# Attention and two mixtures of experts on one core: row maxima split in place on GpSimd, all low weight parts on VectorE, third token tiles transposed whole

## The chip, the cores and the metric

The kernel runs on one core of a Trainium2 chip. The metric is the device time of one execution in microseconds (us), as the median of several runs. TensorE (PE in the profile; PEld is its weight load), VectorE (DVE), ScalarE (ACT), GpSimd (POOL) and SyncE (SP, which issues most DMAs) each work off a queue of their own in order and wait for each other through semaphores.

## The reference

```python
# 1. attention with decay: B=4 batches, 8 heads, 576 positions, 64 columns
cum = cumsum(log(clip(f, 1e-4, 1)))
scores = q @ k.T / 8 + (cum[:, None] - cum[None, :])        # per head, causal
attn = softmax(scores)                                      # with the row maximum subtracted
x = (attn @ v).reshape(2304, 512)
# 2. first mixture of experts: each token goes to its best expert
e = argmax(normalize(x) @ normalize(emb).T / tau);  gate = softmax(...)[e]
x = gate * (relu(x @ w1[e]) @ w2[e])
# 3. second one: (token, expert) pairs by descending logit, at most 288 tokens per expert
logits = x @ w_gate;  assign greedily
out = relu(x @ w1[e]) @ w2[e]
```

Products are done to about fp32 accuracy with pairs: an operand is held as a high part and a low part, and three products (high x high, low x high, high x low) are added up.

## The kernel before

**Attention.** There are 32 heads (batch times head). The loop over heads `n` has six steps `i` per head. In them TensorE does, interleaved: the scores of head n (`st_steps`, lines 545 and 546, into `px`), whose exponentials ScalarE writes (L547) and GpSimd masks (`affine_select`, L552 and L555); the scores of head n+1 once more, for its row maxima (`max_steps`, L509, into two buffers `pl`), which VectorE reduces (L513, L517); and the products with the values of head n-1 (`av_steps`, L578). When the maxima of head n+1 are complete, `rows1` splits them into a high and a low bf16 part in the tile `mb` (VectorE, L523 and L524); at the end of head n `rows` transposes `mb` on TensorE (five 128x128 transposes, L529, into `pr`), and ScalarE copies two rows of the result into rows 96 and 97 of the operand `opA` of head n+1 (L530). So the next head's scores subtract their maximum inside the product. Right behind the transposes TensorE starts the maxima of head n+2.

Operands are prepared two heads ahead by `prep`, in two halves: ScalarE copies a high part (`opA<-raw`, L469), GpSimd subtracts to get the low part (`opB<-raw,opA`, L470), and a DMA brings the high part into the other half of `opB` (L471). `parts` (L478 on VectorE, L480 on GpSimd) splits a transposed value tile every second head, and `ven` (L489) uses it behind the odd heads. In the text an odd head is one with `ven` behind its transposes.

**Experts.** `Weights.load` brings a piece of 128x1024 into one of four buffers `wraw` (SP), and `Weights.split` makes two parts of it: `whi` on ScalarE (L858) and `wlo`, by default on VectorE (L859). Each expert has 8 pieces, four for each of its two products. `load_next` issues the next load of a fixed list; as `wraw` has four buffers, a load waits on SP for the split of the piece four before it.

The first expert starts with the tokens whose place is known (`First`, L958, filled in while the router's last choices run), then `Experts.all` runs the eight experts of the first layer (room for 368, 368, 320, 312, 296, 280, 264 and 256 tokens) and later those of the second (288 each). Per expert there are 8 steps of the first product (L1558 into `pl`; ScalarE takes the positive part into `room_hh`, L1561; VectorE the rest into `room_hl`, L1562) and 4 of the second (L1582 into `py`). The tokens of the next expert are gathered by indirect DMA (POOL), at most 128 per tile, and transposed on TensorE beside the second product (`columns`, L1498); the third tile is transposed with its own number of rows (112, 64, 56, 40, 24, 8 or none in the first layer, 32 in the second). Beside an expert's steps the next expert's weights are split and the following ones loaded.

Some pieces of `wlo` go to GpSimd instead: eight around the first expert, and all eight that are made beside the last expert of the first layer for the first of the second:

```python
eng = self.nc.gpsimd if self.cold and p == E - 1 else None
...
W.split(0, 4 + j, self.nc.gpsimd if j % 2 else None)
```

**Between the layers** the second router's rounds (`Clear`) run: a chain of small VectorE operations (L1348 to L1374, ending in `c_cmp`), 20 small products (L1379) and two more VectorE operations. Three rounds are started early, beside the last expert; `finish` ends that expert (its logits, L1652); four rounds and the placing follow. Then GpSimd gathers the first expert's tokens of the second layer (L1785), TensorE transposes them (L874) and the second layer starts. The order of instructions on each engine is that of the code: nothing rearranges it.

## Time and profile before

| what | value |
|---|---|
| median of 3 runs | 843.05 us (835.38 to 844.14) |
| the profiled execution | 839.43 us, its span 837.5 us |
| busy: PE, PEld | 769.0 us (92%), 725.2 us (87%) |
| busy: DVE, ACT, POOL | 540.7 us (65%), 409.3 us (49%), 332.7 us (40%) |
| mean granted TensorE clock | 0.946 |

The stages by the clock of the span: attention to about 260 us, the first expert's start to 330, the first layer to 520, its last expert and the router's rounds to 592, the second layer to 830. Busy shares are averages over these: in the expert layers TensorE is never idle, in the others it is.

### The profile page before, as it was taken

How to read it: one execution, taken by the hardware profiler on the slowest of the kernel's cores; microseconds unless marked ns; L12 is line 12 of the kernel's file. 1: busy time of each engine (PE TensorE's matmuls, PEld its weight loads, DVE VectorE, ACT ScalarE, POOL GpSimd, SP SyncE). 2: the span in 40 equal slices, each digit the busy share in tenths (PEclk: the TensorE clock that was granted, in tenths of full speed). 3: DMA queues.
4: the chain of work that ended last, by engine and by line, in shares of the span. 5: the costliest groups of instructions: out<-in, count | busy, mean ns of one | idle time of the engine just before them, and what ended most of it. 6: DMA issues, size and time to landing. Idle time of an engine off the chain costs nothing. (4 is left out here: it accounts for less than half of the span.)

```text
span 837.5 us, 16417 instructions
## 1 busy us (share of the span) xinstructions
PE 769.0 (92%) x5813; PEld 725.2 (87%) x5813; DVE 540.7 (65%) x1362; ACT 409.3 (49%) x898; POOL 332.7 (40%) x659
## 2 busy tenths in 40 slices
PE   6899999999998798999999999654999999999995
PEld 2799999899898798999999999653799999999993
DVE  8888988858986668464565467866345554555530
ACT  5556656546656445455455567210344455454520
POOL 8686666546664737621132111810311312231011
PEclk8999999869999999999999999865899999999998
DMA  6466656536554436454555563520445655665410
GB/s 147 103 156 155 152 145 155 142 97 152 140 163 142 159 119 204 148 173 145 178 168 172 187 190 104 169 74 2 119 152 186 203 176 181 200 187 176 126 35 29
DMA packets 70256, 121.75 MB, mean 145 GB/s; under 512 B 29499, under 2 KB 38715, under 8 KB 70165
## 3 DMA queue, kind: packets, MB, share of 16 engines
q1 hardware_dynamic: 63924, 101.24, 43.0%
q0 software_dynamic: 6240, 19.36, 6.3%
q8 instruction: 50, 0.82, 0.4%
q14 instruction: 42, 0.34, 0.1%
HBM read 96.46 MB, written 14.63 MB: 133 GB/s over the span
## 5 line engine op out<-in xcount | busy, mean ns | idle before, releaser
L859 DVE TENSOR_TENSOR wlo<-wraw,whi 128x1024 fp32r<-128x1024 f32 x112 | 142.2, 1270 | 131.6 <-ACT whi L858 130.5
L858 ACT ACTIVATE whi<-wraw 128x1024 fp32r<-128x1024 f32 x128 | 134.6, 1056 | 4.3 <-DMA wraw<-v 3.6
L470 POOL TENSOR_TENSOR opB<-raw,opA 64x576 fp32r<-64x576 f32 x64 | 91.5, 1430 | 68.5 <-ACT opA L469 66.9
L1561 ACT ACTIVATE room_hh<-pl 128x288 fp32r<-128x288 f32 (+8 forms) x128 | 52.0, 406 | 106.3 <-PE pl L1558 105.8
L1558 PE MATMUL pl<-room_xh,whi 128*128 128x288 f32 (+7 forms) x512 | 94.4, 306 | 6.7 <-DVE room_hl L1562 6.2
L1562 DVE SCALAR_TENSOR_TENSOR room_hl<-pl,room_hh 128x288 fp32r<-128x288 f32 (+8 forms) x128 | 57.1, 448 | 53.9 <-ACT room_hh L1561 53.6
L1582 PE MATMUL py<-room_hh,wlo 128*128 128x288 f32 (+7 forms) x480 | 91.7, 315 | 0.0
L1558 PE MATMUL pl<-room_xl,whi 128*128 128x288 f32 (+7 forms) x512 | 90.2, 298 | 1.4 <-DVE room_xl L1501 1.4
L1558 PE MATMUL pl<-room_xh,wlo 128*128 128x288 f32 (+7 forms) x512 | 89.8, 297 | 0.0
L1558 PEld LDWEIGHTS pl<-room_xh,whi 128*128 128x128 f32 x512 | 75.7, 190 | 8.3 <-DVE room_hl L1562 7.4
L1558 PEld LDWEIGHTS pl<-room_xl,whi 128*128 128x128 f32 x512 | 76.0, 189 | 1.9 <-DVE room_xl L1501 1.7
L1582 PE MATMUL py<-room_hh,whi 128*128 128x288 f32 (+7 forms) x480 | 76.8, 303 | 0.0
L509 PE MATMUL pl<-opA 96*128 96x288 f32 (+2 forms) x192 | 70.6, 373 | 6.3 <-DVE opA L382 3.2
L1582 PE MATMUL py<-room_hl,whi 128*128 128x288 f32 (+7 forms) x480 | 76.4, 302 | 0.0
L1558 PEld LDWEIGHTS pl<-room_xh,wlo 128*128 128x128 f32 x512 | 76.0, 189 | 0.0
L545 PE MATMUL px<-opA 128*128 128x288 f32 (+2 forms) x192 | 74.1, 386 | 0.7 <-ACT opA L530 0.5
L1785 POOL DMA_INDIRECT xg<-y_d,ix x24 | 27.3, 1137 | 116.6 <-PE px L1498 86.1
L1582 PEld LDWEIGHTS py<-room_hh,wlo 128*128 128x128 f32 x480 | 71.2, 191 | 2.1
L513 DVE CUSTOM_DVE_ANT_0 mxs<-pl,mask 128x512 f32<-128x512 f32 (+3 forms) x128 | 61.8, 483 | 16.6 <-PE pl L509 12.8
L578 PE MATMUL py<-vv,room_hl 128*128 128x73 f32 x480 | 71.9, 274 | 0.0
L578 PE MATMUL py<-vv,room_hh 128*128 128x73 f32 x480 | 71.6, 270 | 0.0
L578 PEld LDWEIGHTS py<-vv,room_hl 128*128 128x128 f32 x480 | 69.6, 200 | 0.8
(369 smaller groups left out, 1527.4 us busy)
## 6 DMA issues: line engine op xcount, KB each, us to landing
wraw<-w SPq DMA_DIRECT2D x64, 512.0 KB, 3.6
wraw<-v SPq DMA_DIRECT2D x64, 512.0 KB, 3.5
raw<-qkT SPq DMA_DIRECT2D x32, 288.0 KB, 4.0
opB<-opA SPq DMA_DIRECT2D x64, 144.0 KB, 2.4
vv<-vrow SPq DMA_DIRECT2D x32, 160.0 KB, 3.1
vt<-vT SPq DMA_DIRECT2D x16, 288.0 KB, 4.0
x_d<-xr SPq DMA_DIRECT2D x16, 256.0 KB, 2.7
opA<-chl SPq DMA_DIRECT2D x60, 2.2 KB, 3.3
```

The lines of the kernel that those rows point to most:

```text
L470: nc.gpsimd.tensor_tensor(b_[lo, t, :], raw[:, t, :], r32(a[0:64, t, :]), op=ALU.subtract)
L509: nc.tensor.matmul(p[:, :wp], af[0:96, q0:q0 + 128], a[0:96, 1, k0:k0 + wp], start=True, stop=True)
L513: nc.vector.tensor_tensor_reduce(t[:qw, :w], p[:qw, :w], mask[:qw, m0:m0 + w], 1.0, mx[:qw, 5:6] if col == 4 else -3.0e38, op0=ALU.add, op ...
L545: nc.tensor.matmul(o, af[:, ks], a[:, 0, q1 - wp:q1], start=True, stop=False)
L578: nc.tensor.matmul(p[:, i, :], PT[n % 2][0][:, c:c + 128], v_[:, j, :], start=(k == 0), stop=(k == len(AORD) - 1))
L858: self.nc.scalar.activation(hi, raw, AF.Copy)
L859: (eng or self.nc.vector).tensor_tensor(lo, raw, r32(hi), op=ALU.subtract)
L1558: nc.tensor.matmul(o, a[:, d, f0:f0 + 128], b[:, d, o0:C], start=(n == 0), stop=(n == 11))
L1561: nc.scalar.activation(hh[:, fc, c0:C], o, AF.Relu)
L1562: nc.vector.scalar_tensor_tensor(hl[:, fc, c0:C], o, 0.0, r32(hh[:, fc, c0:C]), op0=ALU.max, op1=ALU.subtract)
L1582: nc.tensor.matmul(o, a[:, fc, :], b[:, fc, :C], start=(n == 0), stop=(n == 23))
L1785: nc.gpsimd.indirect_dma_start(out=g[:w], out_offset=None, in_=y_d, in_offset=IOA(ap=ix2[:w, p * NT + t:p * NT + t + 1], axis=0))
```

## The change

**Row maxima.** `mb` becomes a tile of fp32 (128x5x64, of which the bf16 view has 128 columns). VectorE writes each maximum into column 48 of it, so its high bf16 half stands in bf16 column 97; one GpSimd subtraction of 128x5 writes maximum minus high half, as bf16, over its low half in column 96. The two VectorE instructions L523 and L524 are dropped, and the rows of ones in `opA` change sign. The second half of `prep` moves from step 2 to step 4 of a head.

**Low parts.** `split` is divided in `upper` (ScalarE) and `lower` (VectorE), and no `wlo` is made on GpSimd any more. Beside the last expert of the first layer only four `upper` are made, without loads; their four `lower` come behind the rounds, right after the first gathers of the second layer, each with a load. The other four pieces of that expert are split in steps 0 to 3 of its first product.

**Third tiles** are transposed whole, 128x128, whatever their number of rows. One of them gets a memset of the rows that no gather has filled yet.

```diff
-    MB = [const.tile([128, NCH, 128], BF, name=f"mb{i}") for i in range(2)]
+    MB = [const.tile([128, NCH, 64], F32, name=f"mb{i}") for i in range(2)]
...
     def rows1(n):
-        mx, mb = MX[n % 2][:, 0:NCH], MB[n % 2]
-        nc.vector.scalar_tensor_tensor(mb[:, :, 96], mx, -2.0, mx, op0=ALU.mult, op1=ALU.add)
-        nc.vector.scalar_tensor_tensor(mb[:, :, 97], mx, -1.0, mb[:, :, 96], op0=ALU.mult, op1=ALU.subtract)
+
+        mx = MB[n % 2][:, :, 48:49]
+        nc.gpsimd.tensor_tensor(half(mx, 0), mx, half(mx), op=ALU.subtract)
...
-            nc.tensor.transpose(p[:, i * 128:(i + 1) * 128], MB[n % 2][:, i, :], identb)
+            nc.tensor.transpose(p[:, i * 128:(i + 1) * 128], MB[n % 2][:, i, :].bitcast(BF), identb)
...
-            if i in (0, 2):
+            if i in (0, 4):
                 emit(pp, 1)
...
-    first_expert.split(0, nc.vector)
+    first_expert.split(0)
     first_expert.split(1)
-    first_expert.split(2)
+    first_expert.W.upper(0, 2)
...
     first_expert.slots(u, EARLY // 128, NT)
+    first_expert.W.lower(0, 2)
...
-    def split(self, key, j, eng=None):
-        raw = self.raw.pop((key, j))
+    def upper(self, key, j):
         pool, k, bufs = (self.pool, "1", 4) if j < 4 else (self.pool2, "2", 8)
         hi = pool.tile([128, 1024], F32R, name="whi" + k, bufs=bufs)
         lo = pool.tile([128, 1024], F32R, name="wlo" + k, bufs=bufs)
-        self.nc.scalar.activation(hi, raw, AF.Copy)
-        (eng or self.nc.vector).tensor_tensor(lo, raw, r32(hi), op=ALU.subtract)
+        self.nc.scalar.activation(hi, self.raw[key, j], AF.Copy)
         self.parts[key, j] = (hi, lo)
 
+    def lower(self, key, j):
+
+        hi, lo = self.parts[key, j]
+        self.nc.vector.tensor_tensor(lo, self.raw.pop((key, j)), r32(hi), op=ALU.subtract)
+
+    def split(self, key, j):
+        self.upper(key, j)
+        self.lower(key, j)
+
...
-    def split(self, j, eng=None):
-        self.W.split(0, j, eng or self.nc.gpsimd)
+    def split(self, j):
+        self.W.split(0, j)
...
         for t, w in self.tiles(p):
-            nc.tensor.transpose(q[:, t * 128:t * 128 + w], self.rows[p][t][:w, d * 128:(d + 1) * 128],
-                                self.env["identf"][:w, :w])
+            nc.tensor.transpose(q[:, t * 128:(t + 1) * 128], self.rows[p][t][:, d * 128:(d + 1) * 128],
+                                self.env["identf"])
...
-            eng = self.nc.gpsimd if self.cold and p == E - 1 else None
+
+            last = self.cold and p == E - 1
...
-                    if self.cold and p == 0 and step in LATE:
-                        j = LATE.index(step)
-                        W.split(0, 4 + j, self.nc.gpsimd if j % 2 else None)
+                    if p == 0 and step in LATE:
+                        W.split(0, 4 + LATE.index(step))
                         load_next()
+                    if last and step % 2 == 1:
+                        nW.upper(np_, step // 2)
                     elif nW is not None and step % 2 == 1 and (p or not self.cold):
-                        nW.split(np_, step // 2, eng)
+                        nW.split(np_, step // 2)
                         load_next()
...
     L2 = Experts(nc, env, W2, (CAP,) * E, TAILS2, gather2, sink2, True, False)
     L2.fetch(0)
+
+    for j in range(4):
+        W2.lower(0, j)
+        load_next()
```

The order of GpSimd's instructions in two successive heads of the attention stage, the first an odd one; first before, then after. `mb` holds the maxima, `opB` the low operand parts, `room_h*` the exponentials.

```order
L480 TENSOR_TENSOR cum_118<-cum_118 128x576
L552 AFFINE_SELECT room_hl<-room_hl 128x2x128
L470 TENSOR_TENSOR opB_110<-raw,opA_107 64x576
L552 AFFINE_SELECT room_hl<-room_hl 128x2x128
L555 AFFINE_SELECT room_hl<-room_hl 64x64
L470 TENSOR_TENSOR opB_111<-raw,opA_108 64x576
```

```order
L480 TENSOR_TENSOR cum_118<-cum_118 128x576
L551 AFFINE_SELECT room_hl<-room_hl 128x2x128
L523 TENSOR_TENSOR mb_119<-mb_119 128x5
L551 AFFINE_SELECT room_hl<-room_hl 128x2x128
L470 TENSOR_TENSOR opB_110<-raw,opA_107 64x576
L554 AFFINE_SELECT room_hl<-room_hl 64x64
L470 TENSOR_TENSOR opB_111<-raw,opA_108 64x576
```

The split of the maxima comes between the two masks of 128x2x128, and the second `opB` of a head goes behind the second mask.

ScalarE's order in one head of the attention stage, from the copy of the transposed maxima to that of the next head, before and after. `room_hh<-px` are the exponentials, `opA<-raw` the two copies of `prep`.

```order
L530 ACTIVATE opA_107<-pr 2x576
L547 ACTIVATE room_hh<-px 128x288
L469 ACTIVATE opA_106<-raw 64x576
L547 ACTIVATE room_hh<-px 128x288
L547 ACTIVATE room_hh<-px 128x448
L469 ACTIVATE opA_106<-raw 64x576
L547 ACTIVATE room_hh<-px 128x320
```

```order
L546 ACTIVATE room_hh<-px 128x448
L546 ACTIVATE room_hh<-px 128x320
L626 ACTIVATE sq,ss_1200<-xr 128x448
L546 ACTIVATE room_hh<-px 128x192
L469 ACTIVATE opA_106<-raw 64x576
L546 ACTIVATE room_hh<-px 64x64
```

The second copy moves from behind the 448-column exponential to behind the 192-column one.

VectorE's order at the start of the second layer, from the end of the router's placing (`ix`) on, before and after. `room_xl` belongs to the first expert's tokens, `room_hl` to its first product.

```order
L1446 TENSOR_SCALAR ix_7747<-c_ut 128x24
L1463 UNCONDITIONAL_BRANCH x2
L1461 UNCONDITIONAL_BRANCH
L878 TENSOR_TENSOR room_xl<-px,room_xh 128x288 x2
L878 TENSOR_TENSOR room_xl<-py,room_xh 128x288 x2
L1562 SCALAR_TENSOR_TENSOR room_hl<-pl,room_hh 128x288 x2
L859 TENSOR_TENSOR wlo_8817<-wraw,whi_8816 128x1024
```

```order
L863 TENSOR_TENSOR wlo_7184<-wraw,whi_7183 128x1024
L887 TENSOR_TENSOR room_xl<-px,room_xh 128x288 x2
L887 TENSOR_TENSOR room_xl<-py,room_xh 128x288 x2
L1571 SCALAR_TENSOR_TENSOR room_hl<-pl,room_hh 128x288
L863 TENSOR_TENSOR wlo_8744<-wraw,whi_8743 128x1024
L1571 SCALAR_TENSOR_TENSOR room_hl<-pl,room_hh 128x288
L863 TENSOR_TENSOR wlo_8765<-wraw,whi_8764 128x1024
L863 TENSOR_TENSOR wlo_8771<-wraw,whi_8770 128x1024
L1571 SCALAR_TENSOR_TENSOR room_hl<-pl,room_hh 128x288
```

The first row after is the last of four `wlo` that now stand ahead of `room_xl`, and three more `wlo` stand among the first products: in pairs, one of expert 0 and one of expert 1, from the second product on.

## Rows read from the trace of the kernel before

**Rows 1.** Stretches: us, busy (x instructions) by engine, PEclk, DMA share, GB/s

```profile
160.00:180.00 20.00, 19.03 (x108) 18.61 (x109) 12.13 (x41) 7.59 (x24) 7.65 (x11) 0.58 0.38 97
...
620.00:640.00 20.00, 20.00 (x151) 19.59 (x150) 12.30 (x18) 10.43 (x20) 6.12 (x5) 1.00 0.64 207
...
548.00:552.00 4.00, 4.00 (x29) 4.00 (x29) 0.35 (x2) 0.00 (x0) 0.00 (x0) 0.50 0.19 77
```

**Rows 2.** Waits, 20 to 260 us: waiter <- releaser: us in total, times, longest

```profile
PE pr L529 <- DVE mb L524: 8.4, 14, 1.5
```

**Rows 3.** Groups of equal shape: busy us, mean ns | idle us before them

```profile
L859 DVE TENSOR_TENSOR wlo<-wraw,whi 128x1024 fp32r<-128x1024 f32 x112 | 142.2, 1270 | 131.6 <-ACT whi L858 130.5
...
L470 POOL TENSOR_TENSOR opB<-raw,opA 64x576 fp32r<-64x576 f32 x64 | 91.5, 1430 | 68.5 <-ACT opA L469 66.9
...
L469 ACT ACTIVATE opA<-raw 64x576 fp32r<-64x576 f32 x64 | 42.8, 672 | 0.0
...
L859 POOL TENSOR_TENSOR wlo<-wraw,whi 128x1024 fp32r<-128x1024 f32 x16 | 39.3, 2476 | 17.8 <-ACT whi L858 10.7 <-ACT ohl L1299 7.0
```

**Rows 4.** TensorE, attention: start us, us, instruction [idle before <-releaser]

```profile
62.55 0.44 PE L529 MATMUL pr<-identb,mb 128*128 128x128 bf16 x5
62.80 0.38 PE L509 MATMUL pl<-opA 96*128 96x288 f32 x1
...
69.74 0.45 PE L529 MATMUL pr<-identb,mb 128*128 128x128 bf16 x5 [0.37 <-DVE mb L524]
...
162.89 0.45 PE L529 MATMUL pr<-identb,mb 128*128 128x128 bf16 x5 [0.92 <-DVE mb L524]
```

**Rows 5.** VectorE, the same even head, timeline

```profile
68.43 1.26 DVE L524 SCALAR_TENSOR_TENSOR mb<-mx,mb 128x5 bf16<-128x5 f32 x1
```

**Rows 6.** GpSimd, the odd head ahead of it, timeline

```profile
61.87 0.40 POOL L552 TENSOR_SCALAR_AFFINE_SELECT room_hl<-room_hl 128x256 f32<-128x256 f32 x1
```

**Rows 7.** ScalarE, the last exponentials of these two heads, timeline

```profile
62.19 0.58 ACT L547 ACTIVATE room_hl<-px 128x192 f32<-128x192 f32 x2 [0.46 <-PE px L546]
...
68.84 0.58 ACT L547 ACTIVATE room_hh<-px 128x192 f32<-128x192 f32 x2 [0.46 <-PE px L546]
```

**Rows 8.** TensorE around the first expert, timeline

```profile
265.21 0.18 PE L200 MATMUL px<-oh,before 128*128 128x40 bf16 x1 [2.32 <-DVE oh L647]
...
316.55 0.44 PE L1558 MATMUL pl<-room_xl,whi 128*128 128x368 f32 x1 [1.44 <-DVE room_xl L1501]
```

**Rows 9.** Waits, 256 to 330 us

```profile
PE pl L1558 <- DVE room_hl L1562: 6.0, 2, 4.8
```

**Rows 10.** VectorE around the first expert, timeline

```profile
283.09 6.40 DVE L859 TENSOR_TENSOR wlo<-wraw,whi 128x1024 fp32r<-128x1024 f32 x1 [0.67 <-ACT whi L858]
```

**Rows 11.** TensorE, one transpose group with 112 rows, one with 32, timeline

```profile
297.54 0.48 PE L1498 MATMUL px<-identf,xg 128*128 128x128 f32 x3
297.79 0.92 PE L1582 MATMUL py<-room_hh,wlo 128*128 128x368 f32 x4
...
621.09 0.56 PE L1498 MATMUL px<-identf,xg 128*128 128x128 f32 x3
621.58 0.80 PE L1582 MATMUL py<-room_hh,wlo 128*128 128x288 f32 x4
```

**Rows 12.** Waits, 515 to 556 us

```profile
PE pl L1379 <- DVE c_cmp L1374: 9.5, 3, 5.4
```

**Rows 13.** TensorE, closing logits and an undisturbed round, timeline

```profile
548.63 3.56 PE L1652 MATMUL px<-iw,yT 128*128 128x8 f32 x16
...
562.29 1.38 PE L1379 MATMUL py<-c_oh,c_cmp 128*128 128x8 bf16 x20 [3.80 <-DVE c_cmp L1374]
```

**Rows 14.** GpSimd, a gather in the first layer, timeline

```profile
323.49 1.83 POOL L1687 DMA_INDIRECT xg<-x_d,gix  x1 [0.30 <-DVE c_L L1310]
```

**Rows 15.** DMA issues: KB each, median us from issue to landing

```profile
wraw<-v SPq DMA_DIRECT2D x64, 512.0 KB, 3.5
```

**Rows 16.** ScalarE in the second layer's first expert, timeline

```profile
600.19 0.41 ACT L1561 ACTIVATE room_hh<-pl 128x288 fp32r<-128x288 f32 x1 [0.24 <-PE pl L1558]
```

More of the change, by code (lines that the diff above doesn't have):

```diff
@@ L374, in attention @@
                             fill=-8.0e9, base=0, channel_multiplier=1)
-    MX = [const.tile([128, 6], F32, name=f"mx{i}") for i in range(2)]
-    for m in MX + MB:
+    part4 = const.tile([128, 1], F32, name="mx")
+    for m in MB:
         nc.gpsimd.memset(m, 0.0)
@@ L872, in columns @@
     for t, w in tiles:
+        r = 128 if whole else w
         for d in range(4):
-            nc.tensor.transpose(q[d][:, t * 128:t * 128 + w], rows[t][:w, d * 128:(d + 1) * 128], identf[:w, :w])
+            nc.tensor.transpose(q[d][:, t * 128:t * 128 + r], rows[t][:r, d * 128:(d + 1) * 128], identf[:r, :r])
     c = slice(c0, t * 128 + w)
@@ L1505, in first_columns @@
         self.x = operands(self.env["room"], "x", 4)
-        columns(self.nc, self.env["psum"], self.env["identf"], self.x, self.tiles(0), self.rows[0], 0)
+        columns(self.nc, self.env["psum"], self.env["identf"], self.x, self.tiles(0), self.rows[0], 0, True)
     def top(self, g):
@@ L1633, in beside @@
                     for j in ((0, 1), (2, 4), (3, 5), (6, 7))[step - 8]:
-                        nW.split(np_, j, self.nc.gpsimd if j > 3 else None)
+                        nW.split(np_, j)
                         load_next()
-                elif nW is not None:
-                    nW.split(np_, step - 4, eng)
+                elif nW is not None and not last:
+                    nW.split(np_, step - 4)
                     load_next()
```

23 lines of the change are left out of this document (12 added, 11 removed).

## The prediction

> **What bounds the kernel now.** I read the busy time in stretches of 20 us first. In the expert layers TensorE is busy in 20.00 of 20 us at full clock, and in 160 to 180 us it is busy 19.03 of 20 at a mean clock of 0.58 [rows 1]. So TensorE's instruction stream is the bound, and a change can gain in three ways only: less work on TensorE, fewer gaps in front of it, or a higher clock. An instruction saved elsewhere counts only where it ends one of those gaps. The next view is the list of waits. It gives the gaps their cause: in the attention stage TensorE waits 8.4 us in 14 waits for the split row maxima `mb` [rows 2].
>
> **Row maxima on GpSimd.** Two VectorE instructions per head go, and one GpSimd subtraction of 128x5 comes in. No row shows that form. From the two rows of GpSimd subtractions, 2476 ns for 1024 columns and 1430 ns for 576 [rows 3], a column takes 2.3 ns and about 0.1 us is left over; so 0.1 us is the lower end, and the 1.43 us of the 576 columns the upper. I take 0.3 us, nearer to the lower end, because 5 columns are nearer to none than to 576.
> [...]
>
> When would the result land? In an odd head GpSimd ends its mask at 62.27 [rows 6] and TensorE reached the transposes of `mb` at 62.55 without a wait [rows 4]: 62.27 + 0.3 = 62.57, a tie. In an even head VectorE's second split was locked by the GpSimd subtraction L470: it took 1.26 us at 68.43 and ended at 69.69, and TensorE lost 0.37 us to 69.74 [rows 4, 5]. The new order on GpSimd puts the split ahead of that L470, so this lock goes. What is late next there is VectorE's L478, which now follows the last maximum at once and reads two tiles as well; if it goes first the split starts some 0.8 us after the maximum, at about 69.0, and still lands before 69.37, when TensorE gets there.
>
> The same edit moves the second `opA` copy of head n+2 on ScalarE from behind the 448-column exponential to behind the 192-column one. TensorE's first maximum product of head n+2 (L509) stands right behind the transposes and reads that copy. Odd head: the last two exponentials start at 62.19 and take 0.58 [rows 7]; the copy (672 ns, [rows 3]) now starts between them, at some 62.5, and ends at 63.2, while L509 stood at 62.80 [rows 4]: +0.4 us, and it hides the tie above. Even head: the copy runs from 69.15 to 69.8 by the same reckoning from 68.84 [rows 7]; L509, which follows the transposes by 0.25, could start at 69.63 and now does at 69.8, against 69.99 before (69.74 + 0.25): -0.2 us. Heads with a long gap, as the 0.92 us at 162.89 [rows 4], gain about 0.7. With 15 pairs at +0.2, some six long gaps at -0.7, and +1.5, about one L470 [rows 3], at the start, where the first split queues on GpSimd behind two of them, the sum is about **0**. Ends: -7, if the copy always lands in time and most of the 8.4 us goes; +10, if every head pays 0.3 us more.
>
> **The clock in attention.** The stretch 160 to 180 us has a mean clock of 0.58 [rows 1], that is 8.4 us of full-speed work missing there, and a little more just after it: 9 us in all. The drop begins right after the 0.92 us gap at 162.89 [rows 4]. That gap came of the lock between VectorE and GpSimd and should shrink to some 0.2 us. Gaps as long at other places were not followed by a drop, so I do not hold it for certain: **-9** is counted, with a rival without it.
>
> **Low weight parts on VectorE.** 16 pieces of 2476 ns on GpSimd become 16 of 1270 ns on VectorE [rows 3]. The gain is not this difference: it is that VectorE no longer stands locked. One VectorE piece took 6.40 us at 283.09, beside two on GpSimd [rows 10]. Around the first expert TensorE waited 2.32 us for the router's `oh` and 1.44 for `room_xl` [rows 8], and 6.0 in two waits for `room_hl` [rows 9], 9.8 us together. VectorE takes over 8 pieces here, 8 x 1.27 = 10.2 us, in a stretch of some 70 us in which those locks cost it more than that; one extra piece stands ahead of the router's chain, and takes back 1.3 of the 2.32. The half-clock that follows the longest gap gives about 1 us more. **-9**, between -5 (the chains are late again for half of it) and -11.
>
> In the last expert 8 pieces leave GpSimd, and four of them (`upper` only) have their VectorE half behind the Clear rounds. TensorE waited 9.5 us in three waits for `c_cmp` [rows 12]. Undisturbed, the VectorE chain of a round keeps TensorE waiting 3.80 us [rows 13]; in this stage the last expert's second-layer products stand between two rounds and cover about that much. Then all 9.5 goes. With the gaps go the two half-clock stretches behind them: the closing logits took 3.56 us [rows 13] in a stretch of mean clock 0.50 [rows 1], 1.8 saved, and about as much on the products after the first gap. **-13**, between -8 and -15.
>
> The price comes at the start of the second layer. After Clear, VectorE now makes four `wlo` (4 x 1.27 = 5.1 us) while GpSimd issues the three gathers that the layer waits for. A gather that met a VectorE piece took 1.83 us [rows 14], about 0.9 more than one alone. I take +2 for the three, between +1 and +5.
> [...]
> Then pieces 4 to 7 of expert 0 are split during the first four products, and each frees the buffer for a load of expert 1. The load for piece (1, 0) can be issued only after the low part of piece (0, 4), at about 599.8 on the clock of before, and lands 3.5 us later [rows 15], at 603.3. On ScalarE that piece stands ahead of the third `hh`, which began at 600.19 [rows 16]. That `hh` then starts at about 604.4, 4.2 late. With two `pl` buffers TensorE can run two products ahead and stalls about 3.7 us, then 0.7 at the next pair; 1.5 us are counted for the clock, which fell behind the longest gaps of before too. **+8**, between +3 (the load is quick, the buffers cover it) and +13.
>
> **Whole third tiles.** A partial tile's transpose costs an issue gap: three transposes with a 32-row one take 621.09 to 621.58, 0.49 us from start to start; three with a 112-row one take 0.25 (297.54 to 297.79) [rows 11]. 48 groups have a tile of 8 to 64 rows. If a whole tile behaves as the 112-row one, 48 x 0.24 = **-11.4** on an engine that has no gap there [rows 1]. Lower end 0, if the gap belongs to the third transpose as such.
>
> **Sum** against the profiled execution of 839.4: 0 - 9 - 9 - 13 + 8 - 11.4 = -34.4, so **805 us**. The runs lie around that execution, 835.4 to 844.1, so no offset is added. What a measurement of this kernel can tell from no change is about 1%, 8.4 us.
>
> **Rivals.**
> A. The clock falls in attention all the same. For it: the long gaps elsewhere show that a drop is not tied to one row, and the runs differ by 9 us. Against: every gap gets shorter. 805 + 9 = 814.
> B. The gap of the third transpose stays. For it: the trace has no group of three full tiles to read. Against: 112 rows have none. 805 + 11 = 816.
> C. The maxima come late in every head: slower than before. If the 128x5 form costs 1.43 us, it ends in an odd head at 62.27 + 1.43 = 63.7, 1.15 late, and in an even one, behind L478, at 70.4, 0.6 later than before; 31 heads x 0.9 = 28 us. Waits of this size stand ahead of the half-clock stretch of before, so that drop stays (9) and a second one comes (9): 805 + 28 + 18 = 851. It decides from an average of 1.1 us late per head on (34.4 / 31), or 0.5 with two drops. Against it: nothing on GpSimd with so few columns is near 1.4 us by the rows.
> [...]
> D. The stall at the start of the second layer is the larger end, or the gains of the two expert stages are the smaller ends: 815 to 822.
>
> **How the numbers follow.** The forecast has 0.52, A 0.25, B 0.08, C 0.05, D 0.10. From the forecast's own ends (the attention term and the second layer mostly, 788 to 816) the range goes up to A, B and most of D: 788 to 822. Faster by over 1% are all but C and the worst of several at once: 0.92; the rest is 0.05 within and 0.03 slower.
>
> **What would show it.** `mb` written by GpSimd in about 0.3 us; a new wait of TensorE's L509 (now L508) for ScalarE's `opA`, 0.2 to 0.4 us a head; full clock from 160 to 185; no VectorE piece over 2 us around 283; no wait for `c_cmp` ahead of the closing logits; the groups of three transposes at 0.25 us; ScalarE waiting for `wraw` of expert 1 soon after the second layer starts. I am wrong if TensorE waits for `mb` in most heads, or if the closing logits, at 548.63 before [rows 13], start much later than 514: that is 9 + 9, the 11.4 of the 13 that lie ahead of them, and the 20 transpose groups of the first layer (4.8) earlier.

## The result and the profile after

The changed kernel takes 811.26 us (median of 4 runs, 811.0 to 813.0) where the kernel before took 839.2 (835.3 to 844.1): a ratio of 0.967, with a 95% interval of 0.960 to 0.974. The profiled executions are 811.05 and 839.43 us, 28.4 apart. The prediction was 805, 34 less. Ratios here leave out runs more than 1.5% above the fastest of their kernel; where TensorE's clock falls in some executions and not in others, medians and spreads of all runs are given beside them.

The pages of the kernel before and of the changed one, their 40 slices: busy tenths of TensorE and its granted clock.

```profile
PE   6899999999998798999999999654999999999995
...
PEclk8999999869999999999999999865899999999998
```

```profile
PE   3799999999999899999999999925799999999995
...
PEclk9999999999999999999999999855899999999998
```

The two slices of the attention at 8 and 6 tenths of the clock are gone, and TensorE starts later: its first slice is 3 and was 6. By this row the clock is still low (8, 5, 5 and 8 tenths) only in the rounds between the two expert layers, up to the start of the second. The same stretches as in [rows 1], changed kernel:

```profile
160.00:180.00 20.00, 19.50 (x172) 18.32 (x171) 16.09 (x60) 13.05 (x38) 12.65 (x20) 1.00 0.53 134
...
548.00:552.00 4.00, 3.93 (x22) 2.21 (x22) 3.02 (x11) 0.00 (x0) 0.00 (x0) 0.50 0.01 4
```

160 to 180 us now runs at full clock with 172 matmuls where 108 were. (548 to 552 us is another place of the program now; there the rounds still run at half clock.)

Where the 28 us come from is read from TensorE's timeline: the start of the first instruction of each stage, in us.

| stage, from its first TensorE instruction to the next one's | before | after | difference |
|---|---|---|---|
| start, to the transposes of the maxima of the loop's second head | 26.96 | 36.01 | +9.1 |
| from there to the same transposes of the last head | 222.65 | 210.52 | -12.1 |
| to the first product of the first expert | 10.36 | 10.36 | 0.0 |
| first layer, to the first product of a round | 260.93 | 246.15 | -14.8 |
| rounds and placing, to the warming matmuls | 67.04 | 53.01 | -14.0 |
| to the second layer's first product (L1558, now L1567) | 6.49 | 10.96 | +4.5 |
| first expert's first layer, to its second (L1582, now L1591) | 13.70 | 20.27 | +6.6 |
| rest of the second layer | 219.59 | 212.27 | -7.3 |

Three rows of this table are losses. Of the first one only the queue of the first split (1.5 us) was foreseen. GpSimd's timeline at the start of the changed kernel:

```profile
0.78 0.20 POOL masks.py:197 MEMSET identf<- 128x128 f32 x1 [0.29 <-POOLq L1888]
8.23 0.28 POOL masks.py:199 TENSOR_SCALAR_AFFINE_SELECT identf<-identf 128x128 f32<-128x128 f32 x1 [7.24 <-issue]
...
25.00 2.85 POOL L470 TENSOR_TENSOR opB<-raw,opA 64x576 fp32r<-64x576 f32 x2
27.93 0.28 POOL L523 TENSOR_TENSOR mb<-mb 128x5 bf16<-128x5 f32 x1
```

GpSimd stands idle for 7.24 us ahead of an AFFINE_SELECT that waits for nothing the profile shows; in the kernel before it began at 1.29. What follows it on GpSimd moves by some 6.9. Another 2.1 us are the first split, which queues behind two L470, as the prediction counted (1.5).

Attention, the waits of 20 to 260 us (waiter, releaser, us in total, times, longest), and the two groups of equal shape that answer to [rows 3]:

```profile
PEld pl L508 <- ACT opA L469: 6.1, 22, 0.3
...
PE pr L528 <- POOL mb L523: 4.8, 4, 3.3
```

```profile
L863 DVE TENSOR_TENSOR wlo<-wraw,whi 128x1024 fp32r<-128x1024 f32 x128 | 156.4, 1227 | 126.3 <-ACT whi L857 122.0 <-DVEq L1470 2.9 <-ACT room_hh L1570 0.3
...
L523 POOL TENSOR_TENSOR mb<-mb 128x5 bf16<-128x5 f32 x32 | 11.2, 350 | 6.8 <-DVE mb L512 6.7
```

The 8.4 us in 14 waits for `mb` [rows 2] are 4.8 in 4, of which 3.3 is the first head's (before, that head waited 1.6 us for another result, `en`, which the 8.4 leave out). In their place stands what the prediction named, a wait for the moved `opA` copy: 22 waits of TensorE's weight load, 0.3 us each. The split takes 0.35 us on the mean (0.3 was taken): 0.21 alone, and 0.66 where it meets VectorE's L478 (timelines of VectorE and GpSimd):

```profile
90.46 0.75 DVE L478 TENSOR_TENSOR cum<-vt 128x576 f32<-128x576 f32 x1
```

```profile
90.63 0.66 POOL L523 TENSOR_TENSOR mb<-mb 128x5 bf16<-128x5 f32 x1 [0.45 <-DVE mb L512]
```

Around the first expert (waits of 256 to 330 us) TensorE's waits for `room_hl` and `room_xl` [rows 8, 9] are gone but for 0.6 us of its weight load; one new wait has come, for the tail's gather (its issue took 1.75 us beside a VectorE subtraction, 0.97 before):

```profile
PE px L883 <- DMA tail<-x_d,gix: 3.1, 1, 3.1
...
PE px L200 <- DVE oh L646: 0.3, 1, 0.3
```

The rounds beside the last expert and the closing logits, TensorE's timeline, against [rows 12, 13]: no idle time ahead of either round, and the logits start at 518.53 where they started at 548.63 (about 514 by the prediction).

```profile
510.16 1.39 PE L1388 MATMUL pl<-c_oh,c_cmp 128*128 128x8 bf16 x20
517.28 1.39 PE L1388 MATMUL pl<-c_oh,c_cmp 128*128 128x8 bf16 x20
518.53 1.71 PE L1663 MATMUL px<-iw,yT 128*128 128x8 f32 x14
```

A group of three whole transposes in the second layer, against the second pair of [rows 11]: 0.24 us from its start to the next instruction, 0.49 before.

```profile
644.47 0.49 PE L1507 MATMUL px<-identf,xg 128*128 128x128 f32 x3
644.71 0.77 PE L1591 MATMUL py<-room_hh,wlo 128*128 128x288 f32 x4
```

The start of the second layer, timelines of GpSimd, TensorE and ScalarE (they answer to [rows 14 to 16]):

```profile
556.65 1.47 POOL L1799 DMA_INDIRECT xg<-y_d,ix  x1 [29.42 <-PEq L1470]
558.43 1.93 POOL L1799 DMA_INDIRECT xg<-y_d,ix  x1 [0.30 <-issue]
560.66 0.89 POOL L1799 DMA_INDIRECT xg<-y_d,ix  x1 [0.30 <-issue]
561.55 1.52 POOL L1818 COPY ix<-ix 32x1 int32<-32x1 int32 x7
```

```profile
561.58 0.44 PE L883 MATMUL px<-identf,xg 128*128 128x128 f32 x2 [1.67 <-DMA xg<-y_d,ix]
565.10 0.69 PE L883 MATMUL px<-identf,xg 128*128 128x128 f32 x2 [2.86 <-DMA xg<-y_d,ix]
...
579.26 1.01 PE L1567 MATMUL pl<-room_xh,whi 128*128 128x288 f32 x4 [4.20 <-DVE room_hl L1571]
```

```profile
576.52 1.06 ACT L857 ACTIVATE whi<-wraw 128x1024 fp32r<-128x1024 f32 x1 [3.47 <-DMA wraw<-v]
```

Two of three gathers take 1.5 and 1.9 us to issue and land late (1.67 and 2.86 us of waiting), ScalarE stands 3.47 us for the load of expert 1's first piece, and TensorE 4.20 for what is queued behind that on ScalarE and VectorE.

### The profile page after: what moved, and what is told of

Same layout as the page of the kernel before. It is cut to its first block, busy times and chain, and to the rows that moved or that the text cites. A ratio compares the mean times of both kernels' runs of the same rounds, so it can differ in the third digit from the quotient of the medians.

```text
span 809.3 us, 16361 instructions
## 1 busy us (share of the span) xinstructions
PE 741.2 (92%) x5813; PEld 707.5 (87%) x5813; DVE 500.6 (62%) x1314; ACT 408.6 (50%) x898; POOL 302.6 (37%) x674
## 5 line engine op out<-in xcount | busy, mean ns | idle before, releaser
L863 DVE TENSOR_TENSOR wlo<-wraw,whi 128x1024 fp32r<-128x1024 f32 x128 | 156.4, 1227 | 126.3 <-ACT whi L857 122.0
L470 POOL TENSOR_TENSOR opB<-raw,opA 64x576 fp32r<-64x576 f32 x64 | 90.5, 1415 | 44.2 <-ACT opA L469 38.1
L1567 PE MATMUL pl<-room_xh,whi 128*128 128x288 f32 (+7 forms) x512 | 94.7, 307 | 4.6 <-DVE room_hl L1571 4.4
L1567 PE MATMUL pl<-room_xl,whi 128*128 128x288 f32 (+7 forms) x512 | 90.5, 299 | 0.0
L1567 PE MATMUL pl<-room_xh,wlo 128*128 128x288 f32 (+7 forms) x512 | 90.0, 298 | 0.0
L1591 PE MATMUL py<-room_hh,wlo 128*128 128x288 f32 (+7 forms) x480 | 89.8, 311 | 0.0
L1567 PEld LDWEIGHTS pl<-room_xh,whi 128*128 128x128 f32 x512 | 76.0, 191 | 6.3 <-DVE room_hl L1571 5.9
L508 PE MATMUL pl<-opA 96*128 96x288 f32 (+2 forms) x192 | 67.8, 358 | 11.2 <-DVE opA L382 4.4
L1567 PEld LDWEIGHTS pl<-room_xl,whi 128*128 128x128 f32 x512 | 76.7, 191 | 0.1
L1567 PEld LDWEIGHTS pl<-room_xh,wlo 128*128 128x128 f32 x512 | 76.2, 190 | 0.0
L1591 PE MATMUL py<-room_hh,whi 128*128 128x288 f32 (+7 forms) x480 | 76.0, 301 | 0.0
L1591 PE MATMUL py<-room_hl,whi 128*128 128x288 f32 (+7 forms) x480 | 75.8, 300 | 0.0
L1799 POOL DMA_INDIRECT xg<-y_d,ix x24 | 29.2, 1215 | 123.4 <-PE px L1507 88.5
L544 PE MATMUL px<-opA 128*128 128x288 f32 (+2 forms) x192 | 71.8, 374 | 0.1
L1591 PEld LDWEIGHTS py<-room_hh,wlo 128*128 128x128 f32 x480 | 70.6, 190 | 0.0
L577 PE MATMUL py<-vv,room_hh 128*128 128x73 f32 x480 | 69.8, 265 | 0.4 <-DVE vv L492 0.4
L1591 PEld LDWEIGHTS py<-room_hh,whi 128*128 128x128 f32 x480 | 69.1, 189 | 0.0
L1591 PEld LDWEIGHTS py<-room_hl,whi 128*128 128x128 f32 x480 | 69.0, 189 | 0.0
```

What stands on the lines that cost most here:

```text
L470: nc.gpsimd.tensor_tensor(b_[lo, t, :], raw[:, t, :], r32(a[0:64, t, :]), op=ALU.subtract)
L508: nc.tensor.matmul(p[:, :wp], af[0:96, q0:q0 + 128], a[0:96, 1, k0:k0 + wp], start=True, stop=True)
L544: nc.tensor.matmul(o, af[:, ks], a[:, 0, q1 - wp:q1], start=True, stop=False)
L577: nc.tensor.matmul(p[:, i, :], PT[n % 2][0][:, c:c + 128], v_[:, j, :], start=(k == 0), stop=(k == len(AORD) - 1))
L863: self.nc.vector.tensor_tensor(lo, self.raw.pop((key, j)), r32(hi), op=ALU.subtract)
L1567: nc.tensor.matmul(o, a[:, d, f0:f0 + 128], b[:, d, o0:C], start=(n == 0), stop=(n == 11))
```

## The experiments

**The three parts alone**, each put into the kernel before. The first is the transposes (one place of two: the first transposes of the second layer change alike; the memset comes with them):

```diff
-  nc.tensor.transpose(q[:, t * 128:t * 128 + w], self.rows[p][t][:w, ...], self.env["identf"][:w, :w])
+  nc.tensor.transpose(q[:, t * 128:(t + 1) * 128], self.rows[p][t][:, ...], self.env["identf"])
```

> The kernel before with the whole third transposes alone. Theory: each third transpose of a group comes 0.24 to 0.25 us earlier (548 ns to 300 ns behind the second), in the same 47 or so groups as in the changed kernel, and nothing else moves: 11 to 12 us less than the kernel before, 827 to 829 us. Rival: the 0.24 us are hidden behind the copies of the columns or the loads of the products that follow, so that the transposes come closer and the products start where they did: within 2 us of the kernel before.

Measured: 823.8 us (820.4 to 831.1), ratio 0.983 (0.977 to 0.989), some 14 less where 11 to 12 were expected; the interval of the ratio, some 9 to 20 us, holds both. The profiled execution is the slowest of the four, 831.07 us, with two falls of the clock in its attention. In the second layer it gives the 7.3 of the changed kernel. In the first layer it gives more than its 20 groups of 0.24: the wait of 4.8 us for `room_hl` [rows 9] is gone too, though the low parts are still on GpSimd. VectorE's piece that took 6.40 us beside two on GpSimd [rows 10] here takes its place just ahead of them:

```profile
289.68 1.22 DVE L859 TENSOR_TENSOR wlo<-wraw,whi 128x1024 fp32r<-128x1024 f32 x1 [0.67 <-ACT whi L858]
```

```profile
291.78 4.75 POOL L859 TENSOR_TENSOR wlo<-wraw,whi 128x1024 fp32r<-128x1024 f32 x2
```

So that wait was one meeting of two instructions: GpSimd's two pieces start 2.1 us behind VectorE's here, and started 0.6 behind it before. The meeting is no chance of one execution: with the maxima alone and with the preparation moved alone (both below) VectorE's piece takes 6.4 us again, and the wait is 4.7 and 4.8. Why the pieces come further apart here is not shown.

The second part is the maxima: the two VectorE operations replaced by one on GpSimd, and the preparation's second half moved. The forecast was 829 to 831 us: 1 us or less for the maxima themselves, 9 to 10 for the clock of 0.58 at 160 to 180 us [rows 1], which goes with them.

```diff
-        nc.vector.scalar_tensor_tensor(mb[:, :, 96], mx, -2.0, mx, op0=ALU.mult, op1=ALU.add)
-        nc.vector.scalar_tensor_tensor(mb[:, :, 97], mx, -1.0, mb[:, :, 96], op0=ALU.mult, op1=ALU.subtract)
+        nc.gpsimd.tensor_tensor(half(mx, 0), mx, half(mx), op=ALU.subtract)
...
-            if i in (0, 2):
+            if i in (0, 4):
                 emit(pp, 1)
```

> The kernel before with the new maxima alone (split in place on GpSimd, second half of the preparation at the fifth step). [...] GpSimd keeps its low parts here, so the first AFFINE_SELECT still starts at 1.3 us. Rival: the fall of the clock hangs on something else of that one execution, and stays or is gone by chance: within 2 us of the kernel before.

Measured: 831.7 us (829.9 to 833.5 in 12 runs) beside 837.7 (829.4 to 852.0 in 23 runs) of the kernel before; ratio 0.994 (0.992 to 0.997). The fall of the clock is gone and the spread of 23 us is one of 4. The gain is smaller than the 8.6 us that the fall took in the one profiled execution, because not every execution of the kernel before has that fall: the mean granted clocks of its 23 runs go from 0.934 to 0.959, those of these 12 from 0.951 to 0.960, and its fastest run is as fast as this kernel.

The third part is the low weight parts. The forecast was 834 us: -12 by the stages of the changed kernel, and +7 for GpSimd's late start, if that belongs to this part; if it belongs to another, 827 us.

```diff
-  first_expert.split(2)                        # L859 on GpSimd
+  first_expert.W.upper(0, 2)                   # ScalarE; VectorE's lower(0, 2) follows behind slots()
...
-                        nW.split(np_, step // 2, eng)      # eng: GpSimd in the last expert
+                        nW.upper(np_, step // 2)           # lower() x4 behind Clear, ahead of the second layer
```

> The kernel before with the low weight parts on VectorE alone. [...]

Measured: 833.0 us (827.6 to 844.2 in 12 runs), ratio 0.995 (0.991 to 1.000). The stages come out near those of the changed kernel: rounds to the warming matmuls 53.2 us (67.0 before), second layer +5.5 and +6.9. And GpSimd's start is late here as well, with the maxima still on VectorE:

```profile
8.48 0.28 POOL masks.py:199 TENSOR_SCALAR_AFFINE_SELECT identf<-identf 128x128 f32<-128x128 f32 x1 [7.49 <-issue]
```

So the late start belongs to this part. In this execution it saves 22 us in the first layer and the rounds, and gives back 6.6 at the start and 12.4 in the second layer.

**The late start.** The kernel before has TENSOR_TENSORs on GpSimd behind the all-reduce; the changed kernel and the low parts alone have none. So one operation that nobody reads is added there. The forecast was that the 7 us move to it from the start, 6 to 7 us less than the changed kernel, 804 to 805 us:

```diff
         nc.gpsimd.partition_all_reduce(A, am, 128, bass_isa.ReduceOp.max)
         yield
+        back = work.tile([128, 1], F32, name="c_back", bufs=1)
+        nc.gpsimd.tensor_tensor(back, A, A, op=ALU.add)
```

> The changed kernel with one 128x1 addition on GpSimd right behind its all-reduce, whose result nobody reads. [...] Rival: the 7 us at the start come from the order of the start (constants, the first loads), and nothing changes: 810 to 812 us.

Measured: 808.5 us (805.8 to 809.9). GpSimd's timeline, at the start and around its all-reduce:

```profile
1.29 0.29 POOL masks.py:199 TENSOR_SCALAR_AFFINE_SELECT identf<-identf 128x128 f32<-128x128 f32 x1 [0.30 <-POOL identf masks.py:197]
...
479.53 0.38 POOL L1336 PARTITION_ALL_REDUCE c_A<-c_am  x1 [6.69 <-DVE room_xl L1512]
486.69 0.18 POOL L1352 TENSOR_TENSOR c_back<-c_A 128x1 f32<-128x1 f32 x1 [6.78 <-issue]
```

The 7 us of idle time have moved from the start of the execution to the operation behind the all-reduce, where nothing waits for GpSimd. In the kernel before they stood ahead of the first `wlo` behind the all-reduce:

```profile
520.93 2.40 POOL L859 TENSOR_TENSOR wlo<-wraw,whi 128x1024 fp32r<-128x1024 f32 x1 [7.04 <-ACT ohl L1299]
```

That settles where the idle time comes from: the first TENSOR_TENSOR or AFFINE_SELECT after the all-reduce pays it (7.04 us in the kernel before, 6.78 here), and if the execution has none, the next execution does (7.24 in the changed kernel, 7.49 with the low parts alone). The kernel before and the changed one have the same two sequencer instructions (MODIFY_POOL_CONFIG) at 1.2 and 1.0 us, ahead of the first AFFINE_SELECT, so the programs begin alike; it starts at 1.29 us in the two traces above whose kernel has such an operation behind the all-reduce, and at 8.23 and 8.48 in the two that have none. Five more traces agree, those of the moved preparation and of the runs of 882.1, 804.8, 794.2 and 800.8 us below: each kernel has such an operation, and TensorE's first product, which waits for `identb`, starts at 2.25 us as in the kernel before; in the changed kernel it starts at 9.18. Not every operation of GpSimd pays: behind the all-reduce of the changed kernel, indirect DMAs and the seven COPYs at 561.55 us run without that wait, as the MEMSETs do at its start.

The time fell by 2.8 us, not by 6 to 7. TensorE's stretches of the changed kernel and of this one say why (us, busy, clock, DMA share, GB/s):

```profile
20.00:24.00 4.00, 3.95 (x12) 0.59 0.00 0
24.00:28.00 4.00, 0.94 (x5) 1.00 0.59 144
```

```profile
20.00:24.00 4.00, 3.13 (x14) 0.50 0.35 95
24.00:28.00 4.00, 4.00 (x18) 0.50 0.16 37
```

With the early start TensorE's granted clock is 0.50 up to some 30 us, and it loses 2.4 us of its 7.4 in the second head (10.14 us long, 7.75 in the changed kernel). Another 1.3 went in the first layer and 0.8 in the second in this execution.

**Which half of the maxima part does it.** The kernel with that addition (808.5 us) serves as the base from here on. First the split moves to VectorE, same operation, same place:

```diff
-        nc.gpsimd.tensor_tensor(half(mx, 0), mx, half(mx), op=ALU.subtract)
+        nc.vector.tensor_tensor(half(mx, 0), mx, half(mx), op=ALU.subtract)
```

> The kernel that took 808.5 us, with the in-place split of the maxima on VectorE instead of GpSimd, at the same place. Theory: the 0.9 us stalls of the kernel before, from which TensorE's clock fell, came from a VectorE operation held up beside GpSimd's 64x576 subtraction; with the split on VectorE at the new places of the preparation such a coincidence comes back in some heads (an operation of 0.2 us takes 0.8 to 1.4), stalls of 0.5 us and more ahead of the transposes appear again, and with them in some executions a fall of the clock: 2 to 8 us more, 810 to 816 us, and a wider spread of the times. Rival: the preparation's later step alone took the stalls away, and it is no matter which engine does the split: within 2 us of 808.5, no stall of over 0.6 us.

Measured: 805.3 us (804.6 to 805.8), faster by 3.2: the theory is wrong. The heads from the second to the last take 210.4 us, as with GpSimd (210.3); the 3 us are the start, where the split no longer queues behind two L470 and the second head takes 7.84 us and not 10.14.

Then the split stays on GpSimd and the preparation goes back:

```diff
-            if i in (0, 4):
+            if i in (0, 2):
                 emit(pp, 1)
```

> The kernel that took 808.5 us, with the second half of the preparation back at the third step of a head instead of the fifth. Theory: GpSimd's subtraction of 64x576 (1.4 us) then lies ahead of the split of the maxima or beside the masks, and the split on GpSimd waits behind it in its queue in some heads: stalls of 0.3 to 1.4 us ahead of the transposes, 2 to 10 us more; the waits for ScalarE's opA at the first score product of a head (22 times 0.3 us) go, so that as little as 0 may be left. Rival: the step of the preparation is of no matter once the split is off VectorE: within 1.5 us of 808.5, or up to 5 us less.

Measured: 882.1 us (858 to 885), far beyond what either theory gave. The split now stands behind L470 in GpSimd's own queue, and TensorE behind the split (timelines of GpSimd and TensorE):

```profile
44.14 1.89 POOL L470 TENSOR_TENSOR opB<-raw,opA 64x576 fp32r<-64x576 f32 x1 [0.23 <-DVE mb L512]
46.11 0.21 POOL L523 TENSOR_TENSOR mb<-mb 128x5 bf16<-128x5 f32 x1
```

```profile
46.38 0.45 PE L528 MATMUL pr<-identb,mb 128*128 128x128 bf16 x5 [1.08 <-POOL mb L523]
```

17 such waits come to 22.7 us, 3.4 of them the first head's, and five slices of the attention stand at 5 tenths of the clock. The heads from the second to the last take 290.8 us where they took 210.3, at a mean granted clock of 0.73, so most of that loss is the clock's. The preparation's move is therefore no detail: on GpSimd the split can't do without it.

The move alone, on the kernel before, with its two VectorE operations:

> The kernel before with nothing but the second half of the preparation moved from the third to the fifth step of a head; the maxima stay on VectorE with their two operations. Theory: the stalls of 0.9 us ahead of the transposes, and the falls of TensorE's clock behind some of them, come from VectorE's split meeting GpSimd's 64x576 subtraction of the preparation at that old place; moved, they are gone without any new split: 828 to 832 us with a spread of 4 us or less, no stall of over 0.7 us on VectorE's mb between 40 and 250 us. Rival: with two operations the split on VectorE still meets GpSimd's subtractions at other heads, the stalls stay, and the time is that of the kernel before, 835 us with a spread of over 10 us.

Measured: 834.1 us (829.9 to 844.4 in 12 runs); ratio 0.997 (0.993 to 1.001), inconclusive as a time. Its trace answers more: the waits of 0.5 to 0.9 us for `mb` are gone from the third head on, but one of 1.95 is there, where VectorE's second operation meets L470 (timelines of VectorE, GpSimd, TensorE):

```profile
218.12 1.40 DVE L524 SCALAR_TENSOR_TENSOR mb<-mx,mb 128x5 bf16<-128x5 f32 x1
```

```profile
218.09 1.39 POOL L470 TENSOR_TENSOR opB<-raw,opA 64x576 fp32r<-64x576 f32 x1 [0.24 <-ACT room_hl L547]
```

```profile
219.57 0.71 PE L529 MATMUL pr<-identb,mb 128*128 128x128 bf16 x5 [1.95 <-DVE mb L524]
```

VectorE's 128x5 operation ends with GpSimd's, 1.40 us for one that takes 0.18 alone. The next head took 11.3 us instead of 7 (clock 0.75 from 219.5 to 240). With one operation in place of two (the kernel of 805.3 us) this meeting does not happen: its split ends as that L470 starts, and the stall is 0.52.

The last corner: one operation on VectorE, with the preparation at the old place.

> The kernel that took 805.3 us (the changed one with the GpSimd addition and the in-place split on VectorE), with the second half of the preparation back at the third step. Theory: on VectorE, the place of the preparation decides whether the split meets GpSimd's 64x576 subtraction; at the old place the single operation is held up for its 1.4 us in about as many heads as the first of the two was before, the stalls of 0.5 to 0.9 us come back at heads 12, 20 and 28 among others, and TensorE's clock falls behind some of them: 808 to 815 us with a spread of over 5 us. Nothing like the 882 us of the split on GpSimd at the old place, where it stood behind that subtraction in GpSimd's own queue in every head. Rival: one operation in place is quick enough by itself, whatever the place: within 2 us of 805.3.

Measured: 800.8 us (797.0 to 802.6), the theory is wrong again, and the other way. The heads take 207.6 us instead of 210.4: at the old place the `opA` copy is early, so the 6.7 us in 24 waits for it are gone, against 3.0 us in 6 waits for `mb`. The first layer is 2.2 us shorter too in this execution. One of the six waits is long:

```profile
214.36 0.45 PE L528 MATMUL pr<-identb,mb 128*128 128x128 bf16 x5 [1.24 <-DVE mb L523]
```

No fall of the clock followed it in this execution; the spread of 5.5 us is wider than the 1.2 of the new place.

| split, full change with the addition | preparation at the third step | at the fifth step |
|---|---|---|
| one operation on GpSimd | 882.1 | 808.5 |
| one operation on VectorE | 800.8 | 805.3 |

**The start of the second layer.** The next expert's pieces in the second half of the first expert's steps. In the kernel of 808.5 us ScalarE waits 3.4 us for the load of the first of them, and the products 4.1 us for `room_hl`. The forecast was that both waits go, with the low clock behind them (0.58 from 579 to 583 us in the changed kernel): 5 to 7 us less, 802 to 803 us.

```diff
+                    elif p == 0 and not self.cold:
+                        if step > 3:
+                            nW.split(np_, step - 4)
+                            load_next()
```

> The changed kernel with the one GpSimd addition behind the all-reduce (the kernel that took 808.5 us), and in the second expert layer's first expert the next expert's first-layer pieces split at steps 4 to 7 instead of 1, 3, 5 and 7. [...] Rival: with both groups of pieces in the second half, ScalarE and VectorE are late there for the copies, or the second layer's weights come late, and the wait only moves: within 2 us of 808.5.

Measured: 803.5 us (803.2 to 803.8), 5.0 less. The first expert's first layer takes 15.2 us where it took 20.0; ScalarE waits 0.5 us for a load instead of 3.4.

The loads behind the first columns in the text:

```diff
     for j in range(4):
         W2.lower(0, j)
-        load_next()
...
     L2.first_columns()
+    for j in range(4):
+        load_next()
```

> The kernel that took 808.5 us, with the four 512 KB loads at the start of the second expert layer issued behind the first columns instead of behind each of VectorE's four subtractions there; the subtractions stay where they are. Theory: the second gather's rows land late because they share the DMA engines with these loads, so that they land some 3.5 us behind the issue and not 5.8, and the first products start 2 us earlier, 10 us behind the warming matmuls instead of 12; what the loads lose has to be seen at the pieces of steps 0 to 3, whose raw tiles are then some 4 us later, so that the time may come out the same or up to 3 us worse. Rival: the gathers wait for GpSimd alone (1.9 us for an issue beside the subtractions): landing stays at 5 to 6 us, the first products at 12.

Measured: 808.4 us, no change, and no answer: SyncE has nothing queued ahead of the loads, so they start when VectorE's subtractions free the raw tiles, 1.1 us behind the warming matmuls (1.5 in the base). The edit moved nothing. As a repeat of its base on another chip it gives the same time within 0.1 us.

The subtractions themselves, moved to both sides of `c_sel`, where VectorE idles 1.3 us:

```diff
+        if self.gap:
+            self.gap.pop(0)()                 # W2.lower(0, j), load_next()
         nc.vector.tensor_scalar(self.sel, p, CAP - 0.5, None, op0=ALU.is_ge)
+        if self.gap:
+            self.gap.pop(0)()
...
-    for j in range(4):
-        W2.lower(0, j)
-        load_next()
```

> The kernel that took 808.5 us (the changed one with the GpSimd addition), with the four subtractions at the start of the second expert layer moved into VectorE's idle time on both sides of c_sel in the second and third round beside the last expert (1.3 us each, for 1.15 us of work), and their loads with them. Theory: what the change lost at the start of that layer comes from these four alone: the gathers take 1.0 us each again and land in 3.5 us, the first products start 6.5 us behind the warming matmuls and not 12, the rounds take the same 47.5 us: 5 to 6 us less, and 1 to 4 more in the first layer, where two loads are there earlier: 799 to 803 us. Rival: the subtractions push c_sel and what hangs on it, and four loads come beside the last expert's: the rounds lengthen by 1 to 5 us, 804 to 808 us; or the gathers stay late for another reason.

Measured: 804.8 us (800.6 to 805.5). GpSimd at the start of the second layer:

```profile
554.63 1.00 POOL L1809 DMA_INDIRECT xg<-y_d,ix  x1 [30.03 <-DVEq L1478]
555.93 0.96 POOL L1809 DMA_INDIRECT xg<-y_d,ix  x1 [0.30 <-issue]
```

The gathers take 1.0 us again, and the first products come 7.1 us behind the warming matmuls, 12.1 in the base: this loss is that of the four subtractions with the loads that they set off. Which of the two makes an issue longer can be read in the changed kernel's trace, over its first and its fourth gather there (us, busy of PE, PEld, DVE, ACT, POOL, clock, DMA share, GB/s):

```profile
556.65:558.12 1.47, 1.47 (x4) 0.44 (x3) 1.47 (x2) 0.00 (x0) 1.47 (x1) 0.50 0.00 0
...
563.22:564.21 0.99, 0.00 (x0) 0.00 (x0) 0.00 (x0) 0.00 (x0) 0.99 (x1) 0.50 1.03 406
```

The first took 1.47 us beside subtractions while nothing was transferred, the other 0.99 beside transfers of 406 GB/s while VectorE stood still. In that whole trace 34 indirect DMAs have no weight subtraction of VectorE beside them and take 0.86 to 1.30 us to issue; 52 have one, and 35 of these take more than that, up to 1.98. So the longer issues are the subtractions'. Why the rows then land later than the longer issue explains is not separated, since the loads moved as well.

The wait of 4.1 us in the first layer is still there, as the pieces are at the old steps. In the profiled execution the rounds took 1.5 us more; 3.0 us of waiting stood at a branch (L1048) where the base waited 2.3 for `c_cmp`, and why is open. So the gathers did what the theory said, and the median is in the rival's range.

**All together.** Addition, split on VectorE, pieces late, subtractions beside `c_sel`, and the third piece of the first expert behind the tail's gather:

```diff
-    first_expert.W.lower(0, 2)
     ut = R.pool.tile([128, E, NT], F32, name="tk_u")
...
     first_expert.last_rows(work)
+    first_expert.W.lower(0, 2)
     first_expert.split(3)
```

> All together on the changed kernel: the GpSimd addition, the maxima split in place on VectorE, the four subtractions beside c_sel, the next expert's pieces at steps 4 to 7 in the second layer's first expert, and the third piece's subtraction at the start of the first layer behind the tail's gather. Theory: the parts add, 808.5 less 3.2 (VectorE), less 5.0 (pieces), less 5.5 (subtractions), less 1 to 2 (tail): 793 to 795 us. Rival: pieces and subtractions take away the same wait for the loads, so that one of them is counted twice: 797 to 799 us.

Measured: 794.2 us (793.2 to 795.1), ratio to the kernel before 0.950 (0.945 to 0.955), 17 us less than the changed kernel and as the sum of the parts had it. The second layer's first products come 6.6 us behind the warming matmuls, and its first expert's first layer takes 13.9, both as before the change; the rest of the layer keeps its 7.3. Only the tail's edit gave nothing: its wait of 3.1 us became one of 2.9 for the third piece. By the table above the preparation at the old place might take another 4 us off; that was not run.

## Why the prediction was right, and by how much it was not

The sum was -34.4 and the profiled executions differ by -28.4. Term by term, from the table of stages:

- **Row maxima, 0.** -1.4: the heads take 12.1 us less, 8.6 of it the clock, so 3.5 come from the maxima, and 2.1 are lost at the start. The mechanism was right (22 waits of 0.3 us for `opA` in place of the lock, in which VectorE's second operation took 1.26 us beside L470 [rows 5]), the sizes near. What the prediction did not see is that the engine was of no use: one operation in place on VectorE is faster than on GpSimd (805.3 against 808.5 us), and the preparation had to move only for GpSimd's sake.
- **The clock, -9.** The two heads behind 162.89 [rows 4] took 22.4 us and a pair like them 13.7: 8.6. It did go, and rival A did not come. But 9 us is the price of one fall in one execution; over many executions the whole part is worth 6 by medians, 5 by the ratio.
- **Low parts, first expert, -9.** -14.8 less 20 groups of 0.24 is -10. The whole transposes alone took away the longest of these waits as well: the first layer is 11.1 us shorter with them alone, 7.9 with the low parts alone, and 14.8 with both. So the two terms were not independent, and the agreement is partly luck.
- **Low parts, last expert, -13.** -14.0, and with the low parts alone the stage is the same. Right.
- **Start of the second layer, +8.** +11.0: 6.6 where 5.9 were counted for the stall behind the load, and 4.5 where 2 were counted for the gathers. They take 1.5 and 1.9 us beside the subtractions, as the 1.83 of [rows 14] let expect, and 1.00 and 0.96 without them (the run of 804.8 us); but they also land late. This term was undersized by 3.
- **Whole third tiles, -11.4.** Nearly all of the 52 groups of three take 0.24 to 0.25 us; -4.8 in the first layer and -7.3 in the second. (48 x 0.24 is 11.5; 11.4 was counted.) Right, and rival B fell.
- **Missing: +6.9 at the start.** No step of the prediction asked what GpSimd's last TENSOR_TENSOR behind the all-reduce was good for. The sign was in the rows: of the idle time ahead of GpSimd's `wlo` 7.0 us are put down to L1299 on ScalarE [rows 3], in one piece. By the run with the addition it costs the kernel 2.8 us, since the later start gives back 2.4 by the clock in the second head and some 2 in the two expert layers.

6.9 + 3.0 for the second layer, less 3.7 that the other terms together gave more than counted, are about the 6 us between 805 and 811; the time came out nearer than the terms did because these partly cancel. Rival C, maxima late in every head, did not come, but late maxima are real one edit away: 882 us with the preparation left where it was. The cause there is another than the rival's, the queue behind L470 and not the 128x5 form, which takes 0.2 to 0.7 us in that trace as well. Of rival D the start of the second layer came in part, 11.0 of the 13 at its end.

That the fall of the clock follows long stalls ahead of the transposes is shown only as frequency. In the traces of the kernel before, of the three parts alone, of the moved preparation and of the last corner there are 11 stalls of 0.86 us or more ahead of the transposes from the loop's third head on; the granted clock fell to 0.50 behind 5 of them, for 10 to 20 us each, and did not behind the other 6, one of 1.48 us among these. In the changed kernel and the kernels of 808.5, 805.3 and 794.2 us no stall in that part is over 0.82, and the clock does not fall there.

## What to carry to other kernels

Before GpSimd's last TENSOR_TENSOR or AFFINE_SELECT behind an all-reduce is taken away, look for the idle time that it was absorbing: here it came back at the start of the next execution (7.24 us). When operations of two engines hold each other up, as 0.18 us became 1.40 here, fewer and smaller operations on the engine that has them can do more (800.8 and 805.3 us) than a move to the other engine (882.1 and 808.5), whose own queue then holds the critical operation. Work that is pushed out of a busy stage should go into measured idle time of its new engine, not to the head of the next stage, where gathers and loads start.

## What the runs showed of the hardware that was not expected

- Behind GpSimd's all-reduce 6.78 to 7.49 us of idle time are due, in the four traces read there (the kernel before, the changed one, the low parts alone, the addition). They stand ahead of the next TENSOR_TENSOR or AFFINE_SELECT, not of COPYs, MEMSETs or indirect DMAs, and are carried over into the next execution where no such operation follows (a first AFFINE_SELECT at 8.23 and 8.48 us against 1.29).
- A start that is 7.4 us earlier kept 3 of it: the earlier matmuls ran at a granted clock of 0.50 up to about 30 us, those of the later start only up to about 23.
- The same GpSimd subtraction of 128x5 took 0.21 us alone and 0.66 beside VectorE's two-input operation of 128x576; the same size on VectorE took 0.18 alone and 1.40 beside GpSimd's 64x576.
